# Sliding-window attention in 32-key chunks, ahead of a two-layer projection

## The chip, the cores and the metric

The kernel runs on one core of one Trainium2 chip. The metric is the device time of one execution in microseconds. The times shown for a kernel are the median of several executions, and beside them stands one execution that was taken with the hardware profiler on.

## The reference, cut to what matters

Inputs are `q`, `k`, `v` of shape 8 x 8 x 576 x 64 (batch, heads, positions, width of a head) and two weight matrices of 512 x 2048 and 2048 x 512, all float32.

```python
scores = scale * np.matmul(q, k.transpose(0, 1, 3, 2))
mask = np.abs(pos[:, None] - pos[None, :]) <= 32
scores = np.where(mask, scores, -1000000000.0)
scores = scores - np.max(scores, axis=-1, keepdims=True)
attn = np.exp(scores)
attn = attn / (np.sum(attn, axis=-1, keepdims=True) + 1e-09)
attn_out = np.matmul(attn, v)
# x: 4608 tokens x 512, the heads side by side
h = x @ w_in
g = np.where(h >= 1, h, np.where(h <= -1, 0.0, (h + 1) ** 2 / 4))
out = g @ w_out
```

A query sees only the keys at most 32 positions away. The kernel works in bfloat16 with float32 sums, and leaves the maximum out of the exponential.

## The kernel before, in words

The program is one long loop of 144 **steps** (line 505). A step makes one 256-column piece of the hidden layer for 256 tokens, or, in steps 56 to 135 (`WIDE`), a 128-column piece for 512 tokens: matmuls at line 499 or 524 (tile `hp`), then ScalarE's Relu at line 543 and two VectorE instructions at lines 549 and 550 (or ScalarE's Square at line 546 and one VectorE instruction at line 547) that give `gT`. After them the step runs what `ev` lists for it, and then some **units** of the second product (line 459, tile `op`), which are copied out at line 463 and stored from SyncE's queue. All orders are written by hand (`manual_schedule`); each engine runs its instructions in program order.

**Attention** for one batch of eight heads is cut into pieces that `ev` puts between the steps. The positions of `ev` are listed in `sl` (lines 420 and 421); one such position is called a slot here. Eight heads are held as `y` (four heads) on the free axis and `h` (two halves) on the partitions, with 64 partitions for a head's width. There are nine chunks of 64 keys in a head. A chunk's keys can be seen by 128 queries: its own 64 and 32 on each side.

- `scores` (line 215) computes, for two heads `a` on the output partitions and two halves `h` on the input partitions, the 64 x 128 scores of four chunks: sixteen matmuls at line 231, each on a 64 x 64 tile of the array, into a two-bank PSUM tile from the pool `ps_s`. Then comes one ScalarE Exp of 128 x 1024 (line 239), one VectorE multiplication of all of it with a mask of zeros and ones (line 205), and one VectorE addition (line 244) of the even and the odd chunks' weights where they overlap, into `both`, so that the sums over keys need one matmul there and not two. `scores8` (line 246) does the ninth chunk.
- `sums` (line 273) multiplies the weights with the values (`vn`, 64 keys on the partitions) and with ones, on 64 x 64 tiles too, into a two-bank tile from the pool `ps_n` (line 304). Its `end` takes Ln and Exp on ScalarE (lines 310, 311: the reciprocal) and leaves the last multiplication into `xT` (lines 316, 319) to be issued by `flush` in the next step.
- A batch takes five slots. Each slot runs one `sums` and right behind it the `scores` that the next slot's `sums` will need.
- Batch 0, and the batch 1 pieces up to step 13, are masked on TensorE instead: `add_mask` (line 207) first writes a large negative bias with four matmuls, and the scores are added to it.

**Loads.** All loads of `q`, `k`, `v` and of the weights are issued from GpSimd's queue. They use eight semaphores in turn, so an issue waits until the load eight before it has landed. `load_v` (line 103) takes a batch's values in four loads of 64 partitions. At the start the order is: the first halves of `k`, the values of batch 0, five pieces of `w_in`, the second halves of `q` and `k`, ten more pieces of `w_in`, then `w_out`, and batch 1. From batch 2 on `q` and `k` are turned by DMA transposes on SyncE's queue (`xpose`, line 196); a buffer that a load writes is free only once the transpose that read it has landed.

**The start.** Lines 371 to 382 run the first scores and sums of batch 0; `keep_warm` fills gaps in TensorE with matmuls of zeros.

Of the kernel before, what the change touches and what calls it, by code (L numbers as in the profile page):

```python
# [14 lines left out]
def kernel(  # L15
# [19 lines left out]
    nc = tc.nc  # L35
# [3 lines left out]
    NC = S // 64  # L39
    NU = NY * S // 128  # L40
    MAIN = 480
    TAIL = S - MAIN
    CUT = 224
    RING = 4 * S
    PAD = 32
    WIDE = 56, 136
    LONG = 2
# [9 lines left out]
    ps_s = ctx.enter_context(tc.tile_pool(name="ps_s", bufs=1, space=bass.MemoryType.PSUM))  # L57
    ps_n = ctx.enter_context(tc.tile_pool(name="ps_n", bufs=1, space=bass.MemoryType.PSUM))
# [8 lines left out]
    mask4 = const.tile([128, 8 * 128], BF, name="mask4")  # L67
    mask8 = const.tile([128, 4 * TAIL], BF, name="mask8")
# [4 lines left out]
    qTs = [const.tile([128, PAD + NY * S], BF, name=f"qT{i}") for i in range(3)]  # L73
# [6 lines left out]
    HD = (slice(0, 64), slice(64, 128))  # L80

# [21 lines left out]
    def load_v(b, n):  # L103
        if b not in vn:
            vn[b] = nat.tile([128, 2 * NC, 2, D], BF, name="vn", tag="vn", bufs=3)
        h, a = divmod(n, 2)
        y = NY * h + 2 * a
        nc.gpsimd.dma_start(out=vn[b][64 * a:64 * a + 64, :, h], in_=v[b, y:y + 2].rearrange("y s d -> (y s) d")  # L108
                            .rearrange("(c r) d -> r c d", r=64))
# [27 lines left out]
    for n in range(1, 4):  # L137
        load_v(0, n)
# [16 lines left out]
    put([(load_v, 1, n) for n in range(4)])  # L155
    P.tensor_copy(band[HD[1], 0:128], band[HD[1], 64:192])
    for m, n, x in ((mask4, 8, 128), (mask8, 4, TAIL)):
        P.tensor_copy(m.rearrange("p (n j) -> p n j", n=n),
                      band[:, :x].rearrange("p (n j) -> p n j", n=1).to_broadcast([128, n, x]))
    put([(load_w_out, 1, 8 * n, 8 * n + 8) for n in range(2)])  # L160
    put([(load_nat, 2, t) for t in range(2)] + [(load_v, 2, n) for n in range(4)])
# [4 lines left out]
    def qkT(b, t):  # L166
        if t == 0:
            return qTs[b % 3][:, PAD:]
        if b not in kT:
            kT[b] = ktp.tile([128, NY * S], BF, name="kT")  # L170
        return kT[b]
# [29 lines left out]
    pt, pt8, both = {}, {}, {}  # L201

    def mask(eng, p, m):
        if eng is not None:
            eng.tensor_mul(p, p, m)  # L205

    def add_mask(ps, n, w):
        for a in range(2):
            for h in range(2):
                nc.tensor.matmul(ps[h][HD[a], :n * w].rearrange("p (n j) -> p n j", n=n), ident[HD[h], HD[h]],  # L210
                                 bias[HD[h], 64 * h:64 * h + w].rearrange("p (n j) -> p n j", n=1)
                                 .to_broadcast([64, n, w]),
                                 start=True, stop=False, skip_group_check=True)

    def scores(b, ys, pars, cs, eng, pool=ps_s, w=128, ready=None):

        if b not in pt:
            pt[b] = ptp.tile([128, 2, 2, 2, 512], BF, name="pt")
        ps = ready or two_banks(pool)
        n = 0  # L220
        if eng is None and not ready:
            cols = (ys[1] - ys[0]) * (pars[1] - pars[0]) * (cs[1] - cs[0])
            add_mask([ps[:, h] for h in range(2)], cols, w)
        for y1 in range(*ys):
            for par in range(*pars):
                for c2 in range(*cs):
                    c = 2 * c2 + par
                    for a in range(2):
                        for h in range(2):
                            s0 = S * (y1 + 2 * a) + 64 * c  # L230
                            nc.tensor.matmul(ps[HD[a], h, w * n:w * n + w], kT[b][HD[h], s0:s0 + 64],  # L231
                                             qTs[b % 3][HD[h], PAD + s0 - 32:PAD + s0 - 32 + w],
                                             start=eng is not None, stop=True, skip_group_check=True)
                    n += 1
        p = pt[b][:, :, ys[0]:ys[1], pars[0]:pars[1], 128 * cs[0]:128 * cs[1] - 128 + w]
        m = 2 if n > cs[1] - cs[0] else 1
        p = p[:, :, ys[0] - ys[0]] if ys[1] - ys[0] == 1 else p[:, :, :, 0]
        like = "p h (y j) -> p h y j"
        A.activation(p, ps[:, :, :w * n].rearrange(like, y=m), AF.Exp, scale=D ** -0.5)  # L239
        mask(eng, p, mask4[:, :256 * n].rearrange("p (h j) -> p h j", h=2).rearrange(like, y=m))  # L240
        if b:
            lo, hi = ((32, CUT), (CUT, MAIN))[cs[0] // 2]
            r = both[b, ys[0], cs[0] // 2] = ptp.tile([128, 2, MAIN - CUT], BF, name="both", bufs=4)
            V.tensor_add(r[:, :, :hi - lo], pt[b][:, :, ys[0], 0, lo + 32:hi + 32], pt[b][:, :, ys[0], 1, lo - 32:hi - 32])

    def scores8(b, eng, pool=None):

        p = pt8[b] = ptp.tile([128, 2, 2, TAIL], BF, name="pt8")
        if pool:
            ps = [pool.tile([128, 2 * TAIL], FP, name="s8", tag="op") for h in range(2)]  # L250
        else:
            bb = two_banks(ps_s)
            ps = [bb[:, h, :2 * TAIL] for h in range(2)]
        if eng is None:
            add_mask(ps, 2, TAIL)
        for y1 in range(2):
            for a in range(2):
                for h in range(2):
                    s0 = S * (y1 + 2 * a) + MAIN
                    nc.tensor.matmul(ps[h][HD[a], TAIL * y1:TAIL * y1 + TAIL], kT[b][HD[h], s0 + 32:s0 + TAIL],  # L260
                                     qTs[b % 3][HD[h], PAD + s0:PAD + s0 + TAIL],
                                     start=eng is not None, stop=True, skip_group_check=True)
        like = "p h y j -> p h (y j)"
        if pool:
            for h in range(2):
                A.activation(p[:, h].rearrange("p y j -> p (y j)"), ps[h], AF.Exp, scale=D ** -0.5)
        else:
            A.activation(p.rearrange(like), bb[:, :, :2 * TAIL], AF.Exp, scale=D ** -0.5)
        mask(eng, p, mask8.rearrange("p (h y j) -> p h y j", h=2, y=2))
# [3 lines left out]
    def sums(b, y1, lo, hi, pool=ps_n):  # L273

        bb = two_banks(pool)
        w = hi - lo
        todo = []
        if lo < MAIN:
            ys, D0 = (y1,), w
            for par in range(2):  # L280
                a0 = max(lo, 32 * par)
                off = 32 - 64 * par
                if b == 0 or (lo == 0 and par == 0):
                    todo.append((None, a0 - lo, (hi if b == 0 else 32) - lo, lambda a, h, par=par, a0=a0, off=off: (
                        pt[b][HD[a], h, y1, par, a0 + off:(hi if b == 0 else 32) + off])))
                if b and par:
                    todo.append((None, a0 - lo, hi - lo, lambda a, h, n=hi - a0: both[b, y1, lo // CUT][HD[a], h, :n]))
                for c2 in range(4):
                    q0, q1 = max(0, 128 * c2 - off, lo), min(128 * c2 + 128 - off, hi)
                    if q0 < q1:  # L290
                        todo.append((NC * y1 + 2 * c2 + par, q0 - lo, q1 - lo, lambda a, h, par=par, q0=q0, q1=q1, off=off: (
                            pt[b][HD[a], h, y1, par, q0 + off:q1 + off])))
        else:
            ys, D0 = (0, 1), 2 * w
            todo.append((None, 0, 2 * w, lambda a, h: pt8[b][HD[a], h].rearrange("p y j -> p (y j)")))
            for y in ys:
                todo.append((NC * y + 8, y * w, y * w + w, lambda a, h, y=y: pt8[b][HD[a], h, y]))
                for c in (None, NC * y + 7):
                    todo.append((c, y * w, y * w + 64, lambda a, h, y=y: pt[b][HD[a], h, y, 1, 448:512]))
        for n, (c, c0, c1, p) in enumerate(todo):  # L300
            o = D0 if c is None else 0
            for a in range(2):
                for h in range(2):
                    nc.tensor.matmul(bb[HD[h], a, o + c0:o + c1], ones[HD[a]] if c is None else vn[b][HD[a], c, h],  # L304
                                     p(a, h), start=n == 0, stop=True, skip_group_check=True)

        def end():
            lr = smp.tile([128, 2, 256], FP, name="lr", bufs=1)
            rc = smp.tile([128, 2, 256], FP, name="rc")
            A.activation(lr[:, :, :D0], bb[:, :, D0:2 * D0], AF.Ln)  # L310
# [286 lines left out]
```

## Time and profile before

| what | value |
|---|---|
| median of three executions | 307.34 us (306.3 to 307.7) |
| the profiled execution: its own time | 307.01 us |
| its span, first to last instruction | 305.2 us |
| granted TensorE clock over the span | 1.000 |
| TensorE matmuls, and weight loads beside them | 3268 each |
| loads of `v`: number, KB each, mean time of an issue on GpSimd | 32, 144 KB, 893 ns |

Times inside the profile are microseconds from the first instruction. PE is TensorE's matmuls, PEld its weight loads, DVE VectorE, ACT ScalarE, POOL GpSimd, SP SyncE. A matmul's duration in the trace holds its whole way through the array, and consecutive matmuls overlap: 512 columns are given as 379 ns, while the next one starts some 216 ns later. What a matmul costs is therefore read from starts, not from durations.

### The profile page before, as it was taken

The page shows a single profiled execution, that of the slowest core. Times are in us where ns is not written, and L with a number is a line of the kernel's source. Part 1 is how long each engine was busy: PE and PEld are TensorE (multiplying, and loading weights), DVE is VectorE, ACT ScalarE, POOL GpSimd, SP SyncE. Part 2 cuts the span into 40 slices and gives each one's busy share as a digit, 9 for nine tenths or more (in the row PEclk, how much of TensorE's full clock was granted, in tenths as well). Part 3 has the DMA queues.
Part 4 walks back from the last instruction along what each step waited for, and adds up shares of the span by engine and source line. Part 5 has one row for each costly group of instructions (what it writes and reads, how often), then busy time and mean ns, then how long its engine had stood idle before and what let it go on. Part 6 is the DMA issues. An engine that isn't in the chain of part 4 may idle for free.

```text
span 305.2 us, 7779 instructions
## 1 busy us (share of the span) xinstructions
PE 296.6 (97%) x3268; PEld 172.1 (56%) x3268; DVE 232.4 (76%) x377; ACT 208.0 (68%) x347; POOL 77.5 (25%) x93
## 2 busy tenths in 40 slices
PE   8889999999999999999999999999999999999995
PEld 3467878876566667545444444444445444446644
DVE  4269878989888898999888878877888877788700
ACT  3677786738877888788877877786778755444311
POOL 8895771019008107303700640000000000000000
PEclk9999999999999999999999999999999999999999
DMA  9999999999999999996999998570101000000121
GB/s 151 182 180 200 187 183 172 173 165 147 135 213 90 172 159 128 150 147 121 165 133 156 120 173 82 113 114 34 37 34 38 37 35 37 35 34 34 63 77 69
DMA packets 137251, 35.66 MB, mean 117 GB/s; under 512 B 122240, under 2 KB 132992, under 8 KB 137216
## 3 DMA queue, kind: packets, MB, share of 16 engines
q0 software_dynamic: 103056, 18.06, 80.5%
q1 hardware_dynamic: 34016, 16.81, 27.2%
q8 instruction: 25, 0.41, 0.6%
q10 hardware_dynamic: 144, 0.29, 0.4%
q14 instruction: 10, 0.08, 0.1%
HBM read 36.70 MB, written 9.44 MB: 151 GB/s over the span
## 4 chain that ended last, share of the span: by engine, by line
PE 84%; DMA 4%; DVE 4%; POOL 4%; ACT 2%; issue 1%; POOLq 0%; ACTq 0%
PE op L459 33%; PE hp L524 23%; PE hp L499 14%; PE op L474 5%; PE bb L304 5%; DMA w_in<-in_moe_w_in_dram 4%; POOL w_in L113 2%; PE bb L231 2%; DVE mx L549 1%; PE op L450 1%; POOL vn L108 1%; ACT pt L239 1%; DVE gT L550 1%; PE tp L191 1%; DVE xT L316 1%
## 5 line engine op out<-in xcount | busy, mean ns | idle before, releaser
L543 ACT ACTIVATE rr<-hp 128x512 f32<-128x512 f32 x144 | 85.5, 594 | 68.5 <-PE hp L524 37.7
L459 PE MATMUL op<-w_out,gT 128*128 128x512 bf16 x496 | 127.0, 380 | 0.0
L549 DVE TENSOR_TENSOR mx<-hp,rr 128x512 f32<-128x512 f32 x110 | 75.8, 689 | 26.1 <-ACT rr L543 25.3
L524 PE MATMUL hp<-xT,w_in 128*128 128x512 bf16 x320 | 82.1, 379 | 0.0
L550 DVE SCALAR_TENSOR_TENSOR gT<-rr,mx 128x512 bf16<-128x512 f32 x110 | 76.4, 694 | 3.8
L459 PEld LDWEIGHTS <-gT 128*128 128x128 bf16 x496 | 46.0, 98 | 47.6
L499 PE MATMUL hp<-xT,w_in 128*128 128x256 bf16 x512 | 66.4, 273 | 3.3 <-DMA w_in<-in_moe_w_in_dram 2.1
L499 PEld LDWEIGHTS <-w_in 128*128 128x128 bf16 x512 | 49.1, 98 | 19.0 <-issue 3.2
L524 PEld LDWEIGHTS <-w_in 128*128 128x128 bf16 x320 | 31.2, 98 | 38.2 <-issue 0.9
L100 POOL DMA_DIRECT2D qn<-in_q_dram x12 | 14.6, 1223 | 91.7 <-DMA kT<-kn 89.6
L239 ACT ACTIVATE pt<-bb 128x1024 bf16<-128x1024 f32 (+1 forms) x33 | 32.8, 999 | 3.5 <-PE bb L231 2.2
L547 DVE SCALAR_TENSOR_TENSOR gT<-hp,mx 128x512 bf16<-128x512 f32 x34 | 23.5, 690 | 13.9 <-ACT mx L546 13.6
L108 POOL DMA_DIRECT2D vn<-in_v_dram x32 | 27.5, 893 | 6.1 <-DMA w_out<-in_moe_w_out_dram 3.2
L463 ACT COPY osb<-op 128x512 f32<-128x512 f32 x31 | 18.0, 579 | 12.0 <-PE op L459 11.6
L316 DVE TENSOR_TENSOR xT<-bb,rc 128x512 bf16<-128x512 f32 (+1 forms) x32 | 20.9, 654 | 5.7 <-ACT rc L311 5.6
L311 ACT ACTIVATE rc<-lr 128x512 f32<-128x512 f32 (+2 forms) x40 | 23.5, 588 | 1.3
L310 ACT ACTIVATE lr<-bb 128x512 f32<-128x512 f32 (+2 forms) x40 | 22.0, 550 | 0.2 <-PE bb L304 0.2
L546 ACT ACTIVATE mx<-rr 128x512 f32<-128x512 f32 x34 | 21.4, 630 | 1.1
L205 DVE TENSOR_TENSOR pt<-pt,mask 128x1024 bf16<-128x1024 bf16 (+1 forms) x33 | 20.3, 615 | 1.4 <-ACT pt L239 1.4
L304 PE MATMUL bb<-pt,vn 64*64 64x128 bf16 (+3 forms) x712 | 18.7, 207 | 0.0
L304 PEld LDWEIGHTS <-vn 64*64 64x64 bf16 x712 | 14.7, 107 | 4.9 <-issue 4.7
L474 PE MATMUL op<-w_out,gT 128*128 128x256 bf16 x128 | 16.4, 273 | 0.0
(63 smaller groups left out, 167.2 us busy)
## 6 DMA issues: line engine op xcount, KB each, us to landing
out_dram<-osb SPq DMA_DIRECT2D x35, 256.0 KB, 2.8
vn<-in_v_dram POOLq DMA_DIRECT2D x32, 144.0 KB, 11.2
qn<-in_q_dram POOLq DMA_DIRECT2D x12, 288.0 KB, 6.2
kn<-in_k_dram POOLq DMA_DIRECT2D x12, 288.0 KB, 8.8
w_in<-in_moe_w_in_dram POOLq DMA_DIRECT2D x11, 128.0 KB, 5.1
w_out<-in_moe_w_out_dram POOLq DMA_DIRECT2D x4, 256.0 KB, 9.2
w_out<-in_moe_w_out_dram POOLq DMA_DIRECT2D x2, 512.0 KB, 12.3
kh<-in_k_dram POOLq DMA_DIRECT2D x4, 144.0 KB, 5.1
```

The costliest lines, as they stand in the source:

```text
L108: nc.gpsimd.dma_start(out=vn[b][64 * a:64 * a + 64, :, h], in_=v[b, y:y + 2].rearrange("y s d -> (y s) d") .rearrange("(c r) d -> r c d", ...
L239: A.activation(p, ps[:, :, :w * n].rearrange(like, y=m), AF.Exp, scale=D ** -0.5)
L304: nc.tensor.matmul(bb[HD[h], a, o + c0:o + c1], ones[HD[a]] if c is None else vn[b][HD[a], c, h], p(a, h), start=n == 0, stop=True, skip_g ...
L311: A.activation(rc[:, :, :D0], lr[:, :, :D0], AF.Exp, scale=-1.0)
L316: muls.append(lambda: V.tensor_mul(o, bb[:, :, :D0], rc[:, :, :D0]))
L459: nc.tensor.matmul(op[tt], gT[:, j, home(tt // 2), 128 * (tt % 2):128 * (tt % 2) + 128], w_out[:, j], start=j == 0, stop=j == 15)
L474: nc.tensor.matmul(o[:, tt], gT[:, j, p, 128 * tt:128 * tt + 128], w_out[:, j, 256 * half:256 * half + 256], start=not done, stop=len(done ...
L499: nc.tensor.matmul(hp[:, j], w_in[:, kk, 256 * f + 128 * j:256 * f + 128 * j + 128], xT[:, kk, r0:r0 + TB], start=first and n == 0, stop=l ...
L524: nc.tensor.matmul(hp.rearrange("p n t -> p (n t)"), w_in[:, kk, 128 * f:128 * f + 128], xT[:, kk, r0:r0 + 2 * TB], start=n == 0, stop=n == 3)
L543: A.activation(rr, hp, AF.Relu, scale=0.5, bias=0.5)
L549: V.tensor_max(mx, hp, rr)
L550: V.scalar_tensor_tensor(g, rr, 1.0, mx, op0=ALU.min, op1=ALU.mult)
```

## The change

Keys are taken in chunks of 32 instead of 64: 18 chunks in a head, each seen by 96 queries.

- **Scores** of nine chunks (half a batch, all eight heads) make one slot: 72 matmuls of 96 columns on eight tiles of 64 rows x 32 columns, into four banks. Two Exps follow (960 and 768 columns).
- **The mask** on VectorE covers only the first and the last 32 of each chunk's 96 queries; the middle 32 see all its keys. Two additions over the three overlapping chunks give `tot`.
- **Sums** of a third of a batch (192 queries, all heads) make one slot: eight tiles of 32 rows x 64 columns, one matmul of 192 columns with ones for each tile, then 7 or 8 chunks with 32, 64 or 96 columns each.
- The two pools `ps_s` and `ps_n` are closed at step 24 (`JOIN`), and one pool `ps_a` with a single tile of four banks takes their place; scores and sums use it in turn. The one-slot pairing of sums and scores ends: a batch has two slots for scores and three for sums.
- `load_v` takes a batch in eight loads of 32 partitions. The heads' order in `xT` is unchanged, but the first step's matmuls take them as pairs `2y + m`. Strips at the ends of the buffers for the weights (`pts`) and the queries (`qTs`) are zeroed, and the mask's small tiles are built on VectorE in the start, not on GpSimd.

```diff
-    NC = S // 64
+    KC = 32
+    KW = 3 * KC
+    NC = S // KC
+    MID = NC // 2
+    THIRD = S // 3
+    JOIN = 24
...
-    def load_v(b, n):
+    def load_v(b, n, c0=0, c1=NC):
...
-        nc.gpsimd.dma_start(out=vn[b][64 * a:64 * a + 64, :, h], in_=v[b, y:y + 2].rearrange("y s d -> (y s) d")
-                            .rearrange("(c r) d -> r c d", r=64))
+        y, h = divmod(n, 2)
+        nc.gpsimd.dma_start(out=vn[b][YK[y], c0:c1, h],
+                            in_=v[b, NY * h + y, KC * c0:KC * c1].rearrange("(c r) d -> r c d", r=KC))
...
+    def score(b, ps, c0, c1, eng, ready=False):
+        n = c1 - c0
+        if eng is None and not ready:
+            add_mask(ps, n)
+        for c in range(c0, c1):
+            for h in range(2):
+                for y in range(NY):
+                    s0 = S * y + KC * c
+                    nc.tensor.matmul(ps[YK[y], h, KW * (c - c0):KW * (c - c0) + KW], kT[b][HD[h], s0:s0 + KC],
+                                     qTs[b % 3][HD[h], PAD + s0 - KC:PAD + s0 + 2 * KC],
+                                     start=eng is not None, stop=True, skip_group_check=True)
+
+    def weigh(b, ps, c0, c1, eng):
+        n = c1 - c0
+        p = pts[b % 2][:, c0 + 1:c1 + 1]
+        A.activation(p.rearrange("p c h j -> p h c j"), ps[:, :, :KW * n].rearrange("p h (c j) -> p h c j", c=n), AF.Exp,
+                     scale=D ** -0.5)
+        if eng is not None:
+            p = p.rearrange("p c h (t i) -> p (c h) t i", i=KC)[:, :, 0:3:2]
+            eng.tensor_mul(p, p, mask[:, :2 * n])
+
+    def scores(b, half, eng):
+        bb = four_banks()
+        c0, c1 = ((0, MID), (MID - (b == 0), NC))[half]
+        for fn in (score, weigh):
+            fn(b, bb[0], c0, c0 + 5, eng)
+            fn(b, bb[1], c0 + 5, c1, eng)
+        if b and eng is not None:
...
+            V.tensor_add(s, p[:, m0:m1, :, 2 * KC:], p[:, m0 + 2:m1 + 2, :, :KC])
+            V.tensor_add(s, s, p[:, m0 + 1:m1 + 1, :, KC:2 * KC])
...
+        if b in tot:
+            todo.append((None, lo, hi, lambda y, h: tot[b][YK[y], lo // KC:hi // KC, h]))
+        for c in range(max(lo // KC - 1, 0), min(hi // KC + 1, NC)):
+            q0, q1 = max(lo, KC * c - KC), min(hi, KC * c + 2 * KC)
...
+            todo += [(x, q0, q1, f) for x in ((c,) if b in tot else (None, c))]
...
+            for bb, y, y0 in [(bb, y, y0) for bb, y0, y1 in parts for y in range(y0, y1)]:
+                for h in range(2):
+                    z, x = bb[HD[h], y - y0, o + q0:o + q1], f(y, h)
+                    nc.tensor.matmul(z.rearrange("p (m i) -> p m i", i=KC) if len(x.shape) == 3 else z, ones[YK[y]] if c is None else vn[b][YK[y], c, h],
+                                     x, start=n == 0, stop=True, skip_group_check=True)
+        def end(bb, y0, y1):
+            n = y1 - y0
+            rc = smp.tile([128, NY * TB], FP, name="rc")[:, :n * w].rearrange("p (n t) -> p n t", n=n)
+            A.activation(rc, bb[:, :, w:2 * w], AF.Ln)
+            A.activation(rc, rc, AF.Exp, scale=-1.0)
...
+    for b in range(1, B):
+        third = [(sums, b, THIRD * n, THIRD * n + THIRD) for n in range(3)]
+        seq += [(scores, b, 0), third[0], (scores, b, 1), *third[1:]]
+    sl = [12.5, 14, 16, 18, 20]
+    sl += [27, 29, 31, 33, 36, 39, 42, 45, 48, 51, 54, 57, 60, 63, 66, 69, 72, 75, 79, 83]
+    sl += [86, 89, 93, 97, 101, 105, 109, 113, 117, 121]
...
-                for n in range(4):
+                for n in range(H):
                     load_v(b, n)
```

## The prediction

> **What bounds the kernel now.** I read the page's busy times and its chain of waits first, then the busy time by stage, then the timeline of one slot.
>
> ```profile
> span 305.2 us, 7779 instructions
> PE 296.6 (97%) x3268; PEld 172.1 (56%) x3268; DVE 232.4 (76%) x377; ACT 208.0 (68%) x347; POOL 77.5 (25%) x93
> ...
> PE 84%; DMA 4%; DVE 4%; POOL 4%; ACT 2%; issue 1%; POOLq 0%; ACTq 0%
> ```
>
> TensorE is the bound, but a share of the whole span hides the stages. By stage (span, PE busy, PEld, DVE, ACT, POOL, clock, DMA):
>
> ```profile
> 0.00:26.10 26.10, 21.68 (x376) 13.01 (x376) 13.17 (x30) 17.19 (x28) 21.98 (x37) 1.00 1.41 174
> 26.10:66.00 39.90, 39.88 (x544) 33.05 (x545) 33.72 (x54) 28.57 (x48) 14.26 (x16) 1.00 1.81 176
> 124.00:152.00 28.00, 27.98 (x308) 13.16 (x307) 25.10 (x42) 23.10 (x39) 9.16 (x10) 1.00 1.72 145
> 152.00:222.00 70.00, 70.00 (x684) 33.03 (x682) 56.68 (x91) 51.98 (x86) 8.26 (x8) 1.00 1.00 106
> ```
>
> Until 26.1 us the weights' loads and GpSimd's issues set the pace (GpSimd is busy 21.98 of 26.10 us). After that TensorE has no gaps worth naming, so every nanosecond of TensorE taken from attention comes off the end, unless something else turns up late. Next in line is VectorE, 90% busy from 124 to 152 us. One slot, as PE sees it:
>
> ```profile
> 187.31 1.03 PE L524 MATMUL hp<-xT,w_in 128*128 128x512 bf16 x4
> 188.26 0.21 PE L304 MATMUL bb<-pt,ones 64*64 64x32 bf16 x4
> 188.31 0.27 PE L304 MATMUL bb<-pt,vn 64*64 64x96 bf16 x8
> 188.42 0.25 PE L304 MATMUL bb<-both,ones 64*64 64x192 bf16 x4
> 188.50 0.26 PE L304 MATMUL bb<-pt,vn 64*64 64x128 bf16 x8
> 188.58 0.40 PE L231 MATMUL bb<-qT,kT 64*64 64x128 bf16 x16
> 188.91 1.04 PE L459 MATMUL op<-w_out,gT 128*128 128x512 bf16 x4
> ```
>
> Four dense matmuls take 0.863 us from start to start, so the first four end their turn at 188.17. The slot, 40 small matmuls, costs 188.91 - 188.17 = **0.74 us**. The starts of single instructions in the trace give its parts. Going from dense to tiled costs 93 ns, coming back some 92 ns beyond the last group's columns. Four tiles start 3.3 ns apart. From one group of four to the next it is 42 to 46 ns at 96 columns, 56 at 128, 83 at 192, 28 to 32 at 64 and below (there the weight load decides); the first group of a slot takes 20 more. So a group is paid by its columns, and all four tiles run at once. The five slots of a batch, each measured so, cost 0.74 + 0.74 + 0.74 + 0.78 + 0.64 = 3.65 us, in every batch from 2 on within 0.08; batch 1 costs 4.30.
>
> **The change, part by part.**
>
> *Matmuls.* A batch has 196 now (72 for scores, 124 for sums), in 49 groups of four. After the change it has 144 + 200 = 344, in 43 groups of eight, if eight tiles run at once as four do. A scores slot is nine groups of 96: 93 in + 20 + 8 x 45 + 23 (the last eight starts) + 135 out (40 columns' time + 3 + 92) = 0.63 us. A sums slot at an end of the sequence is 93 + 106 (ones, 192 columns, first group) + 30 + 4 x 45 + 30 + 23 + 108 = 0.57; the middle one has one more group, 0.60. A batch: 2 x 0.63 + 2 x 0.57 + 0.60 = 3.00 us, 0.65 less. The number of slots stays five, so no switches are saved. Six batches give 3.9 us. Batch 1, with its first half masked on TensorE and its first third without `tot`, comes to 0.84 + 0.79 + 0.63 + 0.60 + 0.57 = 3.43, 0.87 less. Batch 0's last sums move behind 26.1 us, some 0.4 us more. Net: **-4.4 us**.
>
> No row shows eight tiles at once. The bounds: the pace of the group of four (45 ns at 96 columns), or twice that, if the array or its read ports serve only four tiles. I take the first, because the four tiles' 3.3 ns between starts leaves room for eight (27 ns) inside 45. Nor does a row show 144 instructions without a pause. TensorE's sequencer is seen at its own semaphore instructions: at 118.30 and 146.59 us 44 instructions ahead of the array, and at 8.51 us with nothing behind it in the queue; from its end at 8.56 to 8.97 us 68 instructions start, 6.0 ns each, with groups as close as in any slot. So feeding costs at most 6.0 ns per instruction, and may cost less than 3; a scores slot would want 100 instructions (144 less the 44 ahead) in 0.38 us, 3.8 ns each. I take it as not binding and keep 6.0 as the other end.
>
> [...]
>
> *VectorE and ScalarE.* Shapes from the groups: 128x1024 bfloat16 686 ns, 512 425 ns, 384 352 ns, thus 164 + 0.51 per column; a mask now takes 490 + 425, the two additions 850 or 980. A batch: masks 1.83, additions 1.83, three last multiplications of 768 columns at 0.97, together 6.6 us against 7.8. ScalarE: Exps of 960 and 768 at 0.97 and 0.81 (from 1022 at 1024 and 490 at 384), Ln and Exp of 768 at 0.79 and 0.84, together 8.5 against 10.3. Neither bounds the end; they save nothing by themselves, and their cover is TensorE's dense work. In one scores slot VectorE gets 1.77 us (before: 686 + 357 + 619 = 1.66), so in the 124 to 152 us stage nothing new waits. If runs of 32 columns lost VectorE's double pace, a scores slot would take 0.9 + 1.8 us more, about 1 us of which would reach `hp`, whose two buffers wait for line 549.
>
> *One tile for scores and sums.* A slot now waits until the last one's four banks are read: two Exps after scores (some 2.4 us after the slot's start), or Ln, Exp and the multiplication of the next step (some 2.8 us). Slots are two steps apart at the least, 3.4 us by the steps at 66 to 80 us. I cost it at nothing; the cover is one step.
>
> *Loads.* Eight loads of `v` for four. An issue of half a load is not shown: between 0.56 us (the same partitions' `qh`, 128 descriptors) and 0.89 (`vn`); I take 0.70, 8 x 0.70 against 3.57, **+2.0 us** on GpSimd ahead of `w_in`. GpSimd already waits there for landings (0.44 at 9.88, 0.61 at 14.92, 1.32 at 25.08), which takes some of it up. I put 0.8 us on the path, between 0 and 2.0. Later:
>
> ```profile
> POOL qn L100 <- DMA kT<-kn: 89.6, 5, 19.6
> ```
>
> GpSimd waits 89.6 us for transposes that free its buffers, so later issues have room. But `kT` of batch 3 lands at 91.9 us, and its first scores start at 94.43; after the change they come at step 39 without a sums in front, near 93. Slack 1 us; I put 0.2.
>
> *The start itself.* Batch 0's first Exps get shorter (1.78 us for 2.3), its sums have 18 groups for 14, VectorE builds masks in some 2 us where it idled until 12.66. I take nothing, with 1 us on each side.
>
> Sum: 307.01 (the profiled execution) - 4.4 + 0.8 + 0.2 = 303.6; that execution is 0.33 under the median of 307.34. Forecast **303.6 us**.
>
> **The rivals.**
>
> *Eight tiles run as two fours (slower).* For: no row shows eight, and the scores' four column tiles need twice the operand streams per row that two do now. Against: starts 3.3 ns apart. Price: 30 groups of 96 columns at +45 ns and 13 others at about +30 are 1.7 us a batch, seven times, 303.6 + 12 = 315.6. It decides from 0.65 us / 43 = 15 ns more per group on.
>
> *TensorE is starved of instructions.* At 6.0 ns a scores slot takes 100 x 6.0 = 0.60 us between its ends for 0.40, sums 0.50 to 0.60 for 0.35 to 0.38: +0.94 a batch, +6.6 in all, 310.2. For: the densest run now needs far less. Against: 68 instructions from an empty queue showed no starving.
>
> *The start or the transposes eat the gain.* All 2.0 us of GpSimd and 1 more at `kT`: 303.6 + 2.0 = 305.6, with later batches each late by as much as TensorE got ahead, 306.3. For: batch 3's slack of 1 us. Against: waits for landings in GpSimd's queue.
>
> *VectorE loses its pace on runs of 32.* 14 scores slots at up to 1 us: 303.6 + 14 = 317. Against: the additions at line 244 keep 425 ns at 512 columns in two strips.
>
> **How the numbers follow.** Forecast 0.60, two fours 0.12, starved 0.12, start or transposes 0.12, VectorE 0.04. A measurement of this kernel tells about 0.5% (1.5 us) from no change. Faster than that is below 305.8: the forecast nearly whole (0.56) and a third of the start case, 0.60. Same takes the forecast's upper edge, most of the start case and a little of starving, 0.15. Slower 0.25. The forecast's own range is 301.2 to 305.6 (the start's bounds and the 42 to 46 ns); reaching to the other cases until two in ten are left, 300.8 to 310.
>
> **What would show it.** Right: slots of about 0.6 us between dense matmuls, eight starts some 3.3 ns apart, groups of 96 columns 42 to 46 ns apart to the end of the slot; PE without gaps after 27 us. Wrong: groups of 96 near 90 ns (two fours); groups that widen only in a slot's second half (starving); a gap before the first scores of batch 3, or `w_in` steps late by 2 us; line 549 late behind masks. If slots cost above 0.73 us each, the forecast is wrong in sign.

## The result: 18 us slower, and the profile after

| | before | after |
|---|---|---|
| median of the runs beside each other, us | 307.08 (4 runs, 306.3 to 307.7) | 325.56 (4 runs, 325.0 to 326.4) |
| profiled execution, us | 307.01 | 325.03 |
| its span, us | 305.2 | 323.2 |
| TensorE instructions (matmul and weight load) | 6536 | 9304 |
| fetches on the instruction queue q8 | 25 | 36 |

The ratio is 1.0606, with an interval of 1.0571 to 1.064. Here and below, ratios and their intervals leave out a run over 1.5% above the fastest of its kernel (one each in e3, e7 and e8), and medians do not. The forecast of 303.6 had the wrong sign, and 325.6 lies far above its range. From the page of the kernel after: the span, the busy times, the granted clock in 40 slices, the queue that carries instructions, and the shares of the chain of waits.

```profile
span 323.2 us, 10536 instructions
PE 305.1 (94%) x4652; PEld 180.6 (56%) x4652; DVE 227.3 (70%) x368; ACT 199.2 (62%) x318; POOL 91.3 (28%) x122
...
PEclk9798799799999999999999999999999999999999
...
q8 instruction: 36, 0.59, 0.7%
...
PE 85%; POOL 4%; issue 4%; DVE 3%; DMA 2%; ACT 1%; POOLq 0%; ACTq 0%
```

TensorE's busy time went up by 8.5 us where some 4 less was forecast, and the span by 18.0. Two things in these lines are new. "issue" has 4% of the chain instead of 1%: time in which an engine waits for nothing that the profile records. And the clock has slices of 7 and 8 in the first fifth of the span, where before it had 9s throughout. The same lines of the page of the kernel before:

```profile
PEclk9999999999999999999999999999999999999999
...
q8 instruction: 25, 0.41, 0.6%
```

How late TensorE's dense work is tells where the time went. Each column is the start of one step's first matmul.

```
step          0      4      6     12     16     20     30     56     72    104    128
before    13.41  22.37  26.12  37.48  46.65  54.96  74.59 124.24 152.52 214.43 260.10
late by     2.1    2.1    7.6    9.5   14.3   15.5   16.8   16.9   17.4   18.1   18.0
```

Fourteen of the 18 us are lost before step 16, thus before 61 us. The steady part, of which most of the forecast was made, loses only some 2.5, and 1.35 of that is one more stop (below). By stage in the kernel after (span, PE busy, PEld, DVE, ACT, POOL, clock, DMA share, GB/s):

```profile
20.00:26.67 6.67, 5.97 (x289) 5.01 (x290) 4.04 (x7) 4.62 (x7) 6.63 (x10) 1.00 1.12 149
26.67:31.82 5.15, 0.20 (x27) 0.10 (x12) 1.55 (x3) 0.00 (x0) 2.19 (x4) 0.82 1.35 183
31.82:35.40 3.58, 3.58 (x25) 2.54 (x25) 1.55 (x3) 2.83 (x5) 1.32 (x2) 0.50 1.24 208
35.40:52.98 17.58, 17.58 (x359) 14.68 (x358) 12.16 (x20) 13.04 (x24) 11.23 (x13) 0.96 1.60 157
52.98:55.91 2.93, 0.23 (x24) 0.10 (x7) 1.69 (x3) 0.42 (x1) 0.66 (x1) 1.00 2.46 159
55.91:60.90 4.99, 4.99 (x97) 3.81 (x98) 2.43 (x4) 2.40 (x5) 1.33 (x2) 0.66 2.19 182
```

In the second row TensorE is idle for nearly all of 5.15 us, ScalarE for all of it and VectorE for 3.6. In the row behind it the clock is 0.50: 3.58 us of work at half speed. The same pair comes again at 52.98 and 55.91. The timeline of TensorE at the first pair (start, duration, what, how many):

```profile
25.40 0.86 PE L272 MATMUL bb<-pt,ones 32*64 32x32 bf16 x80
26.07 0.80 PE L272 MATMUL bb<-pt,vn 32*64 32x32 bf16 x72
31.82 0.25 PE L272 MATMUL bb<-pt,vn 32*64 32x32 bf16 x8 [4.95 <-issue]
```

It stops between the 152nd and the 153rd of the 160 small matmuls of step 4's sums. The 72 before it have read the same tiles. The profile records no semaphore that is waited for and no operand that is late, as if TensorE had no next instruction. There are five such stops:

```
TensorE idle     us     its instruction number    number mod 256
10.99 to 12.60  1.61           446                    190
26.67 to 31.82  5.15          1209                    185
52.98 to 55.91  2.92          1974                    182
62.00 to 62.92  0.92          2230                    182
89.58 to 90.93  1.35          3252                    180
```

Instructions are numbered as the trace records TensorE's matmuls and weight loads; its others, and missing records, are not counted, so the remainder drifts. All five lie at the same place of a 256-instruction piece. With TensorE's own semaphore instructions counted too, which the trace lists, the drift is gone: the five stand at 449, 1217, 1985, 2241 and 3265, which is 193 + 256 k for k = 1, 4, 7, 8 and 12. Queue q8 moves packets of 16384 bytes, and 36 of them for these 9304 instructions make some 256 each. Each stop has one such packet in or just ahead of it: it ends at 11.21 before the resumption at 12.60, at 30.46 before 31.82, at 54.46 before 55.91, at 61.48 before 62.92, at 89.54 before 90.93, some 1.4 us earlier each time. These are the 1st, 4th, 7th, 8th and 12th packets of the queue, so each brings the very piece that the stop waits for. So the reading to test is this: TensorE gets its instructions in pieces of 256 by DMA, and dense runs of small matmuls use up a piece before the next has come.

The steady part has a smaller loss. One scores slot of the kernel after, as TensorE sees it:

```profile
197.43 1.03 PE L497 MATMUL hp<-xT,w_in 128*128 128x512 bf16 x4
198.39 0.78 PE L218 MATMUL bb<-qT,kT 64*32 64x96 bf16 x72
199.09 1.04 PE L431 MATMUL op<-w_out,gT 128*128 128x512 bf16 x4
```

The first four end their turn at 197.43 + 0.86 = 198.29, so the slot costs 0.80 us. Single starts in the trace, in ns from the slot's first matmul:

```
matmuls 1 to 32    starts   0 to 162    eight starts 3.3 ns apart, groups of eight 52 (the first), 43, 42 ns apart
pause                         77 ns
matmuls 33 to 72   starts 239 to 564    8.3 ns per matmul with its weight load, without exception
```

The first 32 matmuls, 64 instructions, run as forecast: eight tiles at once at the pace of four. Then TensorE gets one instruction each 4.17 ns and no more. The sums do the same (32, a pause of 87 to 102 ns, then 8.3 ns each), though their matmuls have other widths, so it is the count and not the columns that sets the place. What makes the pause is open: with 64 instructions ready and 4.17 ns for each further one from the start there would be none. The five slots of a batch cost 0.80 + 0.80 + 0.78 + 0.84 + 0.77 = 3.99 us; 3.65 before, 3.00 forecast.

The sum over the profiled execution: stops 1.61 + 5.15 + 2.92 + 0.92 + 1.35 = 12.0 us; the slow clock behind them 3.58 x 0.50 + 4.99 x 0.34 + 17.58 x 0.04 = 4.2; six batches at 0.34 more, 2.0. Together 18.2, beside 18.0 measured. The sum is rough, and that it closes so well is in part chance. It leaves out the clock of 0.55 behind the first stop (12.60 to 15.50), the other small matmuls of batches 0 and 1, and waits that changed: TensorE waited 2.1 us for `w_in` and 0.9 for `xT` before, 0.4 and nothing after, while its waits for the pieces of `qh` and `kh` grew from 0.3 to 1.6. Nor does it show that the eight loads are free (e7).

### The profile page after: what moved, and what is told of

Read it like the earlier page. It is cut to its first block, busy times and chain, and to the rows that moved or that the text cites. A ratio compares the mean times of both kernels' runs of the same rounds, so it can differ in the third digit from the quotient of the medians.

```text
span 323.2 us, 10536 instructions
## 1 busy us (share of the span) xinstructions
PE 305.1 (94%) x4652; PEld 180.6 (56%) x4652; DVE 227.3 (70%) x368; ACT 199.2 (62%) x318; POOL 91.3 (28%) x122
## 4 chain that ended last, share of the span: by engine, by line
PE 85%; POOL 4%; issue 4%; DVE 3%; DMA 2%; ACT 1%; POOLq 0%; ACTq 0%
PE op L431 32%; PE hp L497 21%; PE hp L470 17%; PE bb L272 5%; PE op L446 5%; PE bb L218 3%; DMA w_in<-in_moe_w_in_dram 2%; POOL vn L109 2%; POOL w_in L114 1%; PE op L422 1%; DVE mx L522 1%; PE tp L188 1%; DVE pt L230 1%; POOL kh L89 1%; ACT rr L516 1%
## 5 line engine op out<-in xcount | busy, mean ns | idle before, releaser
L470 PE MATMUL hp<-xT,w_in 128*128 128x256 bf16 x512 | 68.6, 281 | 0.5 <-DMA w_in<-in_moe_w_in_dram 0.4
L470 PEld LDWEIGHTS <-w_in 128*128 128x128 bf16 x512 | 51.0, 101 | 17.0 <-issue 1.5
L497 PEld LDWEIGHTS <-w_in 128*128 128x128 bf16 x320 | 31.3, 98 | 38.4 <-issue 0.9
L109 POOL DMA_DIRECT2D vn<-in_v_dram x64 | 43.0, 693 | 31.1 <-DMA kn<-in_k_dram 15.4
L281 DVE TENSOR_TENSOR xT<-bb,rc 128x768 bf16<-128x768 f32 (+3 forms) x30 | 23.8, 797 | 22.3 <-ACT rc L279 22.3
L102 POOL DMA_DIRECT2D qn<-in_q_dram x12 | 14.6, 1223 | 73.5 <-DMA kT<-kn 73.5
L226 ACT ACTIVATE pt<-bb 128x960 bf16<-128x960 f32 (+1 forms) x32 | 26.9, 892 | 3.5 <-PE bb L218 1.9
L278 ACT ACTIVATE rc<-bb 128x768 f32<-128x768 f32 (+3 forms) x30 | 20.4, 679 | 13.7 <-PE bb L272 12.4
L272 PE MATMUL bb<-pt,vn 32*64 32x96 bf16 (+2 forms) x1408 | 17.4, 206 | 6.4 <-issue 6.4
L279 ACT ACTIVATE rc<-rc 128x768 f32<-128x768 f32 (+3 forms) x30 | 21.5, 715 | 0.9
L272 PEld LDWEIGHTS <-vn 32*64 32x64 bf16 x1408 | 15.6, 104 | 7.1 <-issue 6.8
L102 POOL DMA_DIRECT2D kn<-in_k_dram x12 | 14.7, 1237 | 0.0
```

What stands on the lines that cost most here:

```text
L102: nc.gpsimd.dma_start(out=x[:, :, h], in_=src[b, NY * h:NY * h + NY].rearrange("y s d -> (y s) d") .rearrange("(u p) d -> p u d", p=128))
L109: nc.gpsimd.dma_start(out=vn[b][YK[y], c0:c1, h], in_=v[b, NY * h + y, KC * c0:KC * c1].rearrange("(c r) d -> r c d", r=KC))
L226: A.activation(p.rearrange("p c h j -> p h c j"), ps[:, :, :KW * n].rearrange("p h (c j) -> p h c j", c=n), AF.Exp, scale=D ** -0.5)
L272: nc.tensor.matmul(z.rearrange("p (m i) -> p m i", i=KC) if len(x.shape) == 3 else z, ones[YK[y]] if c is None else vn[b][YK[y], c, h], x, ...
L470: nc.tensor.matmul(hp[:, j], w_in[:, kk, 256 * f + 128 * j:256 * f + 128 * j + 128], xT[:, kk, r0:r0 + TB], start=first and n == 0, stop=l ...
L497: nc.tensor.matmul(hp.rearrange("p n t -> p (n t)"), w_in[:, kk, 128 * f:128 * f + 128], xT[:, kk, r0:r0 + 2 * TB], start=n == 0, stop=n == 3)
```

## The experiments

Theory A: the stops are TensorE waiting for its next piece of 256 instructions. Theory Q: within a slot, 64 instructions stand ready and the rest come, after a pause, at 4.17 ns each. The expectations name the rivals.

### e1 and e2: small matmuls put into the kernel before

Both take the kernel before and add matmuls of 32 columns into a bank that nothing reads; all of the kernel's own work stays.

```
+    def burst(n, eng):
+        z = two_banks(ps_n)
+        for m in range(n):
+            h, a = divmod(m % 4, 2)
+            nc.tensor.matmul(z[HD[a], h, :32], ones[HD[h]], warm[HD[h], :32], start=True, stop=True, ...)
 e1: +    at(7, (burst, 160))
 e2: +    at(127, (burst, 160))
     +    at(132, (burst, 640))
```

> The kernel before, with 160 small matmuls more (64x64 tiles, 32 columns, on constants, into a free PSUM tile, read by nobody) behind step 7, at some 27 us, where the DMA queues are full. Theory A, TensorE runs out of instructions: they come by DMA in pieces of 16 KB (256 instructions), and a burst of 320 eats more than a piece while the next is stuck behind the loads. Then the burst costs its own 1.6 us (32 pairs at full pace, then 8.3 ns a pair) and a gap of 2 to 5 us, and the clock drops after it: +4 to +8 us, 311 to 315. Theory B, the gaps of the changed kernel come from its own loads, banks or semaphores: no gap here, +1.6 us, 308.7.

> The same on the kernel before, late: 160 small matmuls behind step 127 and 640 behind step 132, where the DMA queues are nearly idle. Own time at 32 pairs of full pace and then 8.3 ns a pair: 1.6 and 5.5 us, +7.1 us together, 314.2, if instructions are always there (theory B). Theory A: the first burst has a gap under 1 us or none, for the next piece arrives fast; the second eats five pieces in 5.5 us and waits some 1 us for most of them: +8 to +13 us in all, 315 to 320.

e1: 309.63 us (10 runs), ratio 1.010 (1.0062 to 1.0137), +2.2 us beside 307.39. The stop is there, 1.53 us from start to start, in the middle of one uniform run:

```profile
27.57 0.84 PE L399 MATMUL bb<-warm,ones 64*64 64x32 bf16 x83
29.76 0.79 PE L399 MATMUL bb<-warm,ones 64*64 64x32 bf16 x77 [1.35 <-issue]
```

It stands at instruction 951, which is 183 past a multiple of 256 (961 and 193 with the semaphore instructions). The size was expected at +4 to +8 and is smaller, and the clock stays at 1.00 behind the stop. By its time alone the run lies nearer to theory B's 308.7; it is the stop in the trace that speaks for A.

e2: 327.75 us (4 runs), ratio 1.0661 (1.0606 to 1.0717), +20.4 us where +8 to +13 was expected. Timeline of the 640 matmuls, and the stages from their start on:

```profile
270.82 1.77 PE L399 MATMUL bb<-warm,ones 64*64 64x32 bf16 x194
274.93 1.89 PE L399 MATMUL bb<-warm,ones 64*64 64x32 bf16 x128 [2.34 <-issue]
278.66 1.90 PE L399 MATMUL bb<-warm,ones 64*64 64x32 bf16 x128 [1.83 <-issue]
282.39 1.90 PE L399 MATMUL bb<-warm,ones 64*64 64x32 bf16 x128 [1.83 <-issue]
285.84 1.04 PE L399 MATMUL bb<-warm,ones 64*64 64x32 bf16 x62 [1.56 <-issue]
```

```profile
270.82:286.81 15.99, 8.42 (x641) 7.96 (x641) 1.86 (x3) 0.60 (x1) 0.00 (x0) 0.63 0.06 20
286.81:292.00 5.19, 5.19 (x19) 1.89 (x14) 0.84 (x2) 0.60 (x1) 0.00 (x0) 0.50 0.01 3
```

This is the clearest picture of the cause. Matmuls come in portions of exactly 128, thus 256 instructions, 3.73, 3.73 and 3.45 us apart, with the DMA engines almost idle (0.06 busy). That is the best steady supply in these runs: 14.6 ns per instruction at 3.73 us, 29 ns per matmul with its weight load. The cost came out above the expectation, since each wait is 1.56 to 2.34 us where some 1 was expected, and since the clock falls to 0.63 and then 0.50, though no stop exceeds 2.6 us. The first burst, of 160, waits too, 1.07 us behind its 138th matmul, where under 1 or none was expected.

### e3: fewer matmuls in the two longest runs of the kernel after

The sums over `ones` of batch 0 from key 256 on, and of batch 1's first half, use the added-up weights `tot`, as those of later batches do. Step 4 has 88 small matmuls instead of 160.

```
-        if b and eng is not None:
+        if True:
```

> The changed kernel, with the two VectorE additions (tot) for batch 0 from key 256 on and for the first half of batch 1 too, so that the sums behind steps 4, 8 and 14 have 88, 32 and 64 matmuls for 160, 48 and 112. Theory A: the gap of 5.15 us behind step 4 and the 2.92 behind step 14 shrink or go, with the slow clock after them: -5 to -10 us, 316 to 320. Theory B: only 136 pairs at 8.3 ns are saved, -1.1 us, 324.4.

319.79 us (4 runs, 318.4 to 325.9), ratio 1.0385 (1.0319 to 1.0451): 5.8 us less than the kernel after, as A expected. The profiled execution is 318.43. Step 4:

```profile
25.26 0.32 PE L272 MATMUL bb<-tot,ones 32*64 32x256 bf16 x8 [0.75 <-DVE tot L246]
25.39 0.24 PE L272 MATMUL bb<-pt,vn 32*64 32x32 bf16 x16
26.53 0.70 PE L272 MATMUL bb<-pt,vn 32*64 32x96 bf16 x64 [0.90 <-issue]
```

The 5.15 us are 1.09, with a wait for `tot` of 0.75 in front. The stop of step 14 is gone. But three others are new, at instructions 2230 (54.53 to 56.73) and 3507 (93.99 to 96.46), and a shorter one from 62.77 to 63.75: less work ahead of a run moves the place where a piece ends in it.

### e8: the same work, 112 instructions further on

This run tells A from any cause that belongs to the work itself. In the idle first microseconds 4 of 11 warm-up matmuls become 60 short ones. Nothing else changes, save where each instruction lies among the pieces.

```
-        keep_warm(11, ps_h, "hp")
+        keep_warm(7, ps_h, "hp", 60)
...
+        for _ in range(short):
+            nc.tensor.matmul(z[:, :32], warm[:, :128], warm[:, :32], start=True, stop=True)
```

> The kernel after, with 112 more TensorE instructions ahead of everything that counts: 4 of the 11 warm-up matmuls of 512 columns become 60 of 32 columns, in the idle first microseconds. The work behind them is unchanged; only the place of each instruction among TensorE's pieces of 256 moves by 112. Theory A (the gaps are TensorE waiting for its next 256 instructions): the gaps stay at places 179 to 190 past a multiple of 256, so they leave their places in the program: not before the 8 last matmuls of step 4's sums (5.15 us) or at the end of step 14's (2.92), but 112 instructions earlier in the program. By the time that 256 instructions take in the trace of after, without its gaps, and 5 us from one piece's start to the next one's arrival, the gaps ahead of 110 us come to 7.0 us in all for 9.8 as it was (12.0 measured): the one in step 4 at 2 to 3 us; the time 320.5 to 324, with some start of its own (up to +1) from the short matmuls. Rival M (the stops belong to their places in the program: a semaphore, vn's or the additions' lateness, the shape of the last group): the gaps stay where they are, 5.15 us ahead of the last 8 matmuls of step 4, and the time stays 325 to 326.5.

```profile
24.34 0.81 PE L272 MATMUL bb<-pt,ones 32*64 32x32 bf16 x80
24.97 0.33 PE L272 MATMUL bb<-pt,vn 32*64 32x32 bf16 x16
29.00 0.83 PE L272 MATMUL bb<-pt,vn 32*64 32x96 bf16 x64 [3.70 <-issue]
```

Step 4 now stops with 64 of its 160 matmuls left instead of 8. That is 56 matmuls, or 112 instructions, earlier in the program: exactly the shift. The stop's number is 1207 (1209 in the kernel after), and the others stand at 1972, 2228 and 3503, of 2.3 to 2.4 us each. So the place is set by the count of instructions and not by the work: rival M is out. In size, step 4's stop is 3.90 us for 5.15, where 2 to 3 were expected, and the four come to 10.8 us, where 7.0 were expected. The first stop, at 11 us, is gone, and step 0 starts at 13.55 (15.51 in the kernel after, 13.41 before). But `w_in` is issued as late as ever, at 8.35 us, and TensorE waits 1.7 us for it inside step 0 and 3.1 in all (0.4 in the kernel after). The time doesn't tell A from M: 323.53 us in the median, but 321.1 to 327.0 over four runs, ratio 1.050 (1.0401 to 1.0599), the profiled execution being the slowest of the four.

### e4: 32 or 40 matmuls at a time

From step 40 on, the dense units that stood behind a scores slot go between its 40 and its 32 matmuls, in the kernel after. They are three or four matmuls of 512 columns (four in the rows below), not the 12 to 16 of the expectation.

```
-        for fn in (score, weigh):
-            fn(b, bb[0], c0, c0 + 5, eng)
-            fn(b, bb[1], c0 + 5, c1, eng)
+        score(b, bb[0], c0, c0 + 5, eng)
+        if mids:
+            mids.pop()()
+        score(b, bb[1], c0 + 5, c1, eng)
+        weigh(b, bb[0], c0, c0 + 5, eng)
+        weigh(b, bb[1], c0 + 5, c1, eng)
```

> The changed kernel, from step 40 on with the step's dense units (12 to 16 matmuls of 512 columns) moved between a scores slot's first 40 and last 32 matmuls. Theory Q, a queue of 64 instructions runs at full pace and then TensorE is fed 4.2 ns per instruction: the first part shows 32 matmuls at 3.3 ns, a pause of some 77 ns and 8.3 ns after it, the second part 32 at full pace, 0.17 us from first to last start; the two cost 0.53 + 0.40 for 0.80 us, nine slots, +1.2 us, 326.7. Rival, eight tiles slow down of themselves (ports, banks): the second part is at 8.3 ns too, or slows after the same number of columns; 327.5.

```profile
202.69 0.51 PE L218 MATMUL bb<-qT,kT 64*32 64x96 bf16 x40
203.13 1.04 PE L434 MATMUL op<-w_out,gT 128*128 128x512 bf16 x4
204.10 0.36 PE L218 MATMUL bb<-qT,kT 64*32 64x96 bf16 x32
204.40 1.04 PE L500 MATMUL hp<-xT,w_in 128*128 128x512 bf16 x4
```

The 32 start within 161 ns of each other, the pace of the first 32 of a whole slot, and without a pause. The 40 take 298 ns: 32 at the full pace, then the pause and eight at 8.3. So 64 instructions stand ready after four dense matmuls, as Q expects, and a slot's last 32 matmuls are not slow of themselves. The two parts cost 0.534 + 0.389 = 0.92 us with two more switches, against 0.80 in one piece, so splitting gains nothing. The time, one run, was 331.93, some 6 us above the kernel after, where 1.2 was expected. From step 44 on TensorE waits in nine places, 5.0 us in all, for VectorE's `mx`, which frees a buffer of `hp`. At 208.31, for one, `mx` had started at 207.57, behind the masks and additions of the scores, and these behind Exps that began only once the last 32 matmuls were done.

### e5 and e6: the first sums too, and half of `v` later

e5 is e3 with `tot` also for the very first sums (80 matmuls instead of 144). e6 is e5 with chunks 9 to 17 of batch 0's `v` loaded behind `w_in`.

```
 e5: +        total(b, half)      (for batch 0's first half called behind both its scores)
     -            m0, m1 = ((0, MID - 1), (MID - 1 if b in tot else THIRD // KC, NC))[half]
     +            m0, m1 = ((0, MID - 1), (MID - 1, NC))[half]
     +        if b == 0:
     +            todo = todo[1:] + todo[:1]
 e6: -    load_v(0, 0)            +    load_v(0, 0, 0, 9)      (and so for n = 1 to 7)
     +    put([(load_v, 0, n, 9, 18) for n in range(H)])      (behind w_in)
```

> The kernel after with `tot` for all of batch 0 and batch 1 (e3 left the very first sums without it): the first sums become 80 small matmuls instead of 144, and the matmuls against `ones` come last there, behind the `tot` additions. In e3 and in the kernel after, TensorE stands still for 1.6 to 2.0 us from about 10.9 us on, at instruction 446 (190 past a multiple of 256), while step 0 starts 2.1 us later than before (15.5 for 13.4). Theory A (TensorE outruns the fetch of its instructions, 256 in 3.7 us at best): the gap at about 11 us falls to under 1 us; the gaps stay at places 179 to 190 past a multiple of 256; if this gap delays step 0, step 0 comes at 13.5 to 14.2 and the time falls by 1 to 2 us against e3, to 316.5 to 319. Rival L (the eight loads of `v` ahead of `w_in` on GpSimd set step 0; first w_in issue 8.55 us for 6.33 before): the gap shrinks but step 0 stays within 0.4 us of 15.5, and the time within 1 us of e3's fast 318.4 to 319.8.

> As e5, but of batch 0's `v` only chunks 0 to 8 are loaded ahead of `w_in` (eight issues of half the rows), and chunks 9 to 17 behind the `w_in` loads. The number of issues ahead of `w_in` stays eight. If rival L holds by the cost of an issue whatever its size (0.69 us each), step 0 stays where e5 has it (within 0.3 us). If by the size of the issue (fewer descriptors, less time on the queue), the first w_in issue moves from 8.55 to some 7 us and step 0 comes 1 to 1.5 us earlier than in e5. Theory A alone expects step 0 unchanged unless the fetches get shorter with less in the queues; more than 1 us gained on e5 would speak for the loads, none against them. Later `v` may cost the second sums (step 4) up to 1 us.

Both missed in time: e5 322.69 us (ratio 1.0471, 1.0387 to 1.0555), e6 327.19 (1.0625, 1.0558 to 1.0692), where 316.5 to 319 was expected of e5. The stop at 11 us did go (0.77 remains, a wait for `tot`). Step 0 comes at 14.62 in e5, as in e3 with its stop (14.56), between what A and what L expected: its weight load waits 1.22 us for `w_in` there, so the loads hold it. In e6 it comes at 13.72, with the first `w_in` issue at 7.75 for 8.41, and the later `v` costs 2.8 us of waits at step 4, where up to 1 was expected. What made both slow lies elsewhere in the main: with 64 matmuls, 128 instructions, fewer ahead, the ends of pieces meet other runs. In e5 the scores near 87 us wait 3.9 us in one place, in e6 5.6 (by the count of instructions others stop for 2.4 and 2.8 us in e5 and 3.2 in e6):

```profile
PE bb L218 <- issue: 3.9, 1, 3.9
```

```profile
PE bb L219 <- issue: 5.6, 1, 5.6
...
PE bb L279 <- DMA vn<-in_v_dram: 2.8, 2, 1.9
```

They stand at instructions 2991 and 2993, 175 and 177 past a multiple of 256, a little outside the 179 to 190 that was named. In these two runs matmul records are missing; counted by their weight loads and the semaphore instructions, both stops stand at 3009, and so 193 past a multiple of 256, as do all such stops of e1 to e8. Their length was not foreseen: at the stops while loads fill the queues a piece arrives 4.0 to 10.4 us after the one before it began to run, and in e2's long burst, with nearly none, 3.5 to 3.7. So fewer small matmuls did not mean less time here (322.69 us in e5, 319.79 in e3): what counted was where the ends of pieces fell. e6's `vn` issues cost 0.61 us for half the rows (4.24 / 7) against 0.69 (4.81 / 7): the price is mostly per issue, so eight cannot be made cheap by making them small.

### e7: the eight loads alone

The kernel before with `v` in eight loads instead of four, nothing else.

```
-        h, a = divmod(n, 2)
-        y = NY * h + 2 * a
...
+        y, h = divmod(n, 2)
+        a, y1 = divmod(y, 2)
...
-    for n in range(1, 4):
+    for n in range(1, H):
```

> The kernel before with one part of the change alone: `v` comes in eight loads per batch (64 partitions by 9 chunks each) instead of four; everything else as before. The forecast put +2.0 us on GpSimd ahead of `w_in` and 0.8 us (0 to 2.0) of it on the path: 308.2 (307.4 to 309.4). Rival L at its full size would give +2 us at step 0 and, if nothing takes it up, 309.4. Theory A expects 0 to 1.5 of the 18 us from it, since TensorE's instruction count is that of before; no gap on TensorE's own instruction fetch beyond those of before.

312.16 us (4 runs, 311.2 to 316.0), ratio 1.0126 (1.0055 to 1.0198): 4.7 us more in the medians, 4.2 between the two profiled executions, and by the interval 1.7 to 6.1; 308.2 was expected. From the chain of waits, and from what TensorE waits for (us in total, times, longest):

```profile
PE 68%; DMA 14%; POOL 8%; DVE 4%; issue 3%; ACT 2%; POOLq 0%; ACTq 0%
```

```profile
PE bb L304 <- DMA vn<-in_v_dram: 1.4, 1, 1.4
...
PE op L474 <- DMA w_out<-in_moe_w_out_dram: 1.0, 1, 1.0
PE bb L231 <- DMA kT<-kn: 0.9, 1, 0.9
PE tp L191 <- DMA kh<-in_k_dram: 0.8, 2, 0.5
```

DMA rises from 4% to 14% of the chain, POOL from 4% to 8%. The lateness grows in pieces: 0.8 us at step 0, 1.7 at step 4, 3.1 at step 16, 4.2 from step 28 on. Each transfer that stands behind the added issues comes late in its turn: batch 0's `v`, its second `kh`, `w_out`, then `kT`. TensorE's instruction count is that of before, and no stop on its instructions is among these waits (thirty gaps of at most 0.2 us that the profile puts to "issue" are places where a matmul record is missing: 3230 matmuls beside 3268 weight loads). An issue of `v` takes 0.77 us in the mean here, 0.69 in the kernel after, whose loads have another shape.

No run beat the kernel before. The best form of the change, e3, is at 1.0385, and by the slots measured, even without any stop, the five slots of a batch at 3.99 us stay 0.34 us behind 3.65.

## Why the prediction was wrong, by its own steps

*Matmuls, eight at once.* Right: eight starts 3.3 ns apart, groups 42 to 43 ns apart at 96 columns behind a first one of 52, where 45 and 65 were taken. The rival of two fours is out.

*Matmuls, feeding.* This is the first of two steps that failed: "I take it as not binding". The bound of 6.0 ns came from 68 instructions behind an empty queue, half of them for scores of 128 columns, which take some 55 ns for a group of four with its weight loads, 7 ns per instruction. Rows that want no more than that could not show a limit of 4.17. Past the 64 that stand ready the rate is 4.17 ns with a pause of 77, so a scores slot is 93 in + 162 + 77 + 40 x 8.3 + 135 out = 0.80 us instead of 0.63. The rival "starved" had this mechanism, its sign (groups that widen only later in a slot) and its price: 3.00 + 0.94 = 3.94 us a batch, 3.99 measured. That the price met is in part luck, since it was made of 100 instructions at 6.0 ns, and not of a pause and 80 at 4.17. The slots also passed the 0.73 us that was named as the turn of the sign. The rival gives 310.2 and so holds 7 of the 22 us between forecast and result.

*What no case had.* The second step that failed is the larger one: that past 26.1 us "every nanosecond of TensorE taken from attention comes off the end", with the supply of instructions put at nothing. It holds the other 15 or so: 12.0 us of stops on the fetch of instructions and 4.2 of slower clock behind them. The trace of before held the clue, in the 25 packets of 16 KB on an instruction queue of its own, but none of its runs is dense enough to show a stop: each packet there lands 1.9 us or more ahead of the first instruction of its piece. The forecast counted what each instruction costs TensorE and never what it costs to bring 2768 more of them, least of all where 160 matmuls stand in a row, in step 4. "PE without gaps after 27 us" was named as the sign of a right forecast; the stop from 26.67 to 31.82 is its plain contrary.

*VectorE and ScalarE.* Without effect on the end, as said; the size was too large: VectorE's busy time fell by 5.1 us and ScalarE's by 8.8, where 1.2 and 1.8 us a batch make 8 and 13 in seven. The Exps were forecast right, at 0.97 and 0.81 us, 0.89 in the mean. Their group and that of `v`'s loads (busy, mean ns, idle before):

```profile
L226 ACT ACTIVATE pt<-bb 128x960 bf16<-128x960 f32 (+1 forms) x32 | 26.9, 892 | 3.5 <-PE bb L218 1.9
...
L109 POOL DMA_DIRECT2D vn<-in_v_dram x64 | 43.0, 693 | 31.1 <-DMA kn<-in_k_dram 15.4
```

*One tile of four banks.* No wait for it shows among TensorE's in the kernel after. It wasn't tried by itself.

*Loads.* The issue was sized right (0.70 us, 693 ns measured), and `w_in`'s first issue came 2.2 us later for 2.0 forecast. What failed is how much of it reaches the end: 0.8 us with 2.0 as the most, against 4.2 to 4.7 in e7, since the slack was taken at one place and is used up at four. In the kernel after, TensorE is so late by itself that these waits are mostly covered; without the first stop some of them appear, as the 3.1 us for `w_in` in e8 and the 1.22 in e5 show.

*The start.* Taken as nothing, within 1 us. Step 0 was 2.1 us late, 1.6 of it the first stop, and the clock was 0.55 behind it; e8, without that stop, has step 0 at 13.55, with the wait for `w_in` inside it.

## What to carry to other kernels

Count instructions as a flow with three rates: what the array takes (a group of eight at 96 columns each 42 to 43 ns here), what the queue is fed (an instruction each 4.17 ns), and what is fetched (256 each 3.73 us in e2). In these runs finer tiles kept the forecast pace only within the 64 instructions that stand ready (32 matmuls with their weight loads), and met no stop only while 256 instructions lasted longer than the fetch of the next 256: 3.5 to 3.7 us with the DMA engines nearly idle, 4.0 to 10.4 at the stops while loads ran. To find such a stop, look for a gap that waits for "issue", count TensorE's instructions up to it, its semaphore instructions too, and see whether the next gap stands a multiple of 256 further on; shifting the program by some cheap instructions settles it.

## What was not expected of the hardware

- TensorE's instructions arrive in pieces of 256, one each 3.73 us with nearly idle DMA engines (e2), and they are not fetched far ahead: in the kernel after, the packet for a piece starts between 3.0 us before and 4.6 us after the first instruction of the piece ahead of it.
- Behind a stop the array often runs at half clock: 0.50 for 3.58 us after 5.15 idle, and 0.50 after e2's stops of 1.8 to 2.5 us with work between them. It is not so behind each: the clock stayed at 1.00 behind 1.53 us in e1 and 1.99 and 2.21 in e3. The five stops of the kernel after, 12.0 us, cost some 4.2 more by it.
- Step 4's stop was 5.15, 3.90 and 1.09 us in the kernel after, e8 and e3 (whose sums are shorter there): the length depends on where a piece ends, which no one had chosen.
